# One quarter of two weight units split into 16 partitions and four transfers of eight partitions

## The chip, the core and the metric

The kernel runs on one core of one Trainium2 chip. The metric is device time in microseconds (us) of one execution. The core has TensorE (PE, matmuls), VectorE (DVE), ScalarE (ACT), GpSimd (POOL) and SyncE (SP). Sixteen DMA engines move data between HBM and the on-chip memory SBUF (128 partitions). POOL and SP each issue transfers into a queue of their own, and the same sixteen engines serve all queues.

## The reference

Causal attention with a decaying bias over 8 batches, 8 heads, 576 tokens and head size 64; then a mix of 64 Fourier modes along the tokens, with a complex 512 by 512 weight matrix for each mode; then a residual with one more product.

```python
scores = scale * np.matmul(q, k.transpose(0, 1, 3, 2))
cum = np.cumsum(np.maximum(s, 0.0), axis=-1)
bias = -(cum[:, :, :, None] - cum[:, :, None, :])
scores = np.where(causal, -1000000000.0, scores + np.minimum(bias, 0.0))
attn_out = softmax(scores) @ v
x = attn_out.transpose(0, 2, 1, 3).reshape(8, 576, 512)
X = np.fft.rfft(x, axis=1)
Xr, Xi = (np.real(X[:, :64]), np.imag(X[:, :64]))
Yr = np.einsum('bmd,mde->bme', Xr, w_r) - np.einsum('bmd,mde->bme', Xi, w_i)
Yi = np.einsum('bmd,mde->bme', Xr, w_i) + np.einsum('bmd,mde->bme', Xi, w_r)
y = np.fft.irfft(Y, n=576, axis=1)
u = x + y
out = u + np.maximum(u @ w_ch, 0.0)
```

The weights `w_r` and `w_i` are 64 by 512 by 512 in float32, 67 MB each. They are read once and stored on chip as bfloat16.

## The kernel before, in words

**Steps.** The attention runs in 32 steps n (L725), one for each pair of heads g (four of them) and batch b (eight). A step computes the scores of two heads, their exponentials (ACT, L513), the product with v (L545), and the forward transform of the step before (L567, L586). Products with the mode weights are put between, from step 8 on: `mode_steps` (L320) gives each step its list, and `mode_products` (L709) runs them at L605. Unit 7 is multiplied in step 14 and unit 12 in step 20. After the attention come the products of the last group g (`modes`, L619, matmuls at L628), the inverse transform, the last product and the stores.

**Weights in units.** For the first three groups g, the weights come in 24 units u. A unit holds 16 modes of the real or of the imaginary weights for the 128 rows of g, as a tile of 128 partitions. `unit_loads` (L249) makes the list of its transfers: four quarters h of 32 partitions each, 512 KB in SBUF and 1 MB in HBM. A destination row holds four blocks j of 2048 elements, (q e) with four q and 512 e. The units use five buffers `w_sb` in turn (L118, L234), but for the first two, which use other tiles. The last group comes in 16 smaller pieces (`tile_loads`, L270), each of two transfers of 64 partitions, and the last piece in four.

**Order of the loads.** `loads_w` (L294) hands out the quarters in order, up to a count; `asked[0]` is how many have been handed out. `on_chip[n]` (L337 to L343) is the count for step n: 3n + 2 from step 8 to step 19, and never past a buffer that a product of this or a later step still has to read (`fits`, L326). In each step, `load` (L311) takes the list of q, k and v loads and the list of weight quarters, places the i-th of l entries at (i + 0.5) / l, sorts by that, and issues all of them on POOL (L315). So a POOL instruction that waits (for a buffer, for instance) holds everything behind it. The transfers that POOL issues use eight semaphores in turn, and a transfer waits until the one eight places ahead has landed.

**SP** issues the small row loads of qt (L441, two rows each), the constants Gx and Gt (L773, L777), and after the last load `mark` (L1040), the spreads of y into yv (L662, 16 partitions each) and the stores.

**At the end**, `modes` of the last mode group waits for the last loads of the weights; then come transposes, products and the stores of the results.

Of the kernel before, what the change touches and what calls it, by code (L numbers as in the profile page):

```python
# [19 lines left out]
def kernel(  # L20
# [15 lines left out]
    P = 128  # L36
# [189 lines left out]
    HU = WM * DM  # L226

    def slot(i, x, n=1):

        return w_sb[i][:, x * WM : (x + n) * WM, :].rearrange("p m e -> p (m e)")  # L230
# [8 lines left out]
    def parts_of(u):  # L239

        if u == 0:
            return [(0, xg[:, : 4 * HU])]
        if u == 1:
            return [(0, ya[:, HU:]), (3, xg[:, 4 * HU : 5 * HU])]
        return [(0, slot(UNIT_AT[u], 0, 4))]

    wt = {}

    def unit_loads(u):  # L249

        g, c, ri = u // NCK, u % NCK // 2, u % 2
        src = (moe_w_r, moe_w_i)[ri][:, g * P : (g + 1) * P, :]
        slots, todo = [], []
        for j0, t in parts_of(u):
            slots += [t[:, i : i + HU].rearrange("p (q e) -> p q e", q=QD) for i in range(0, t.shape[1], HU)]
        for h in range(QD):
            todo.append([])
            for j0, t in parts_of(u):
                first = 1 if ri == 1 and c + h + j0 == 0 else 0
                j1 = j0 + t.shape[1] // HU  # L260
                todo[-1].append((
                    t[QP * h : QP * h + QP, first * HU :].rearrange("p (j x) -> p j x", x=HU),
                    src[16 * c + 4 * (j0 + first) + h : 16 * c + 4 * j1 - 3 + h : 4].rearrange(
                        "j (p q) e -> p j (q e)", q=QD
                    ),
                ))
        wt[g, c, ri] = slots
        return todo

    def tile_loads(k):  # L270

        c, ri = divmod(k, 2)
        src = (moe_w_r, moe_w_i)[ri][:, (NG - 1) * P :, :]
        i, x = TILE_AT[k]
        t = slot(i, 2 * x, 2).rearrange("p (m e) -> p m e", e=DM)
        m0 = 2 * MC * (c // 2) + 2 * (c % 2)
        todo = []
        for x0, x1 in [(0, 4)] if k < NT3 - 1 else [(0, 2), (2, 4)]:
            for h in range(2):
                first = 1 if ri == 1 and c == 0 and x0 + h == 0 else 0  # L280
                todo.append((
                    t[HP * h : HP * h + HP, 2 * (x0 + first) : 2 * x1].rearrange("p (m q) e -> p m (q e)", q=2),
                    src[m0 + 4 * (x0 + first) + h : m0 + 4 * x1 - 3 + h : 4].rearrange(
                        "m (p q) e -> p m (q e)", q=2
                    ),
                ))
        wt[NG - 1, c, ri] = [t[:, :WM], t[:, WM:]]
        n = len(todo) // 2
        return [todo[:n], todo[n:]]

    NLW = 4 * NUN + 2 * NT3
    asked, queued = [0], []

    def loads_w(upto):  # L294
        todo = []
        while asked[0] < min(upto, NLW):
            if not queued:
                t = asked[0]
                queued.extend(unit_loads(t // 4) if t < 4 * NUN else tile_loads((t - 4 * NUN) // 2))
            todo += queued.pop(0)  # L300
            asked[0] += 1
        return todo

    def place_of(t):
# [44 lines left out]
    first = loads_qk(0)  # L349
    load(first[:2])  # L350
    load(loads_w(2 * W0), loads_v(0) + loads_tails(0) + first[2:] + loads_v(1))
    nc.sync.dma_start(out=Ff_sb.rearrange("p T c -> p (T c)"), in_=d_Ff)
    nc.sync.dma_start(out=G_sb[:, :S], in_=d_G)
# [11 lines left out]
    with tc.tile_pool(name="cum_psum", bufs=1, space=PSUM) as cpsum:  # L365
# [29 lines left out]
        for x in range(2):  # L395
            rows = slice(NL * x, NL * x + NL)
# [222 lines left out]
    def modes(g, c, meanwhile=None, ris=(0, 1)):  # L619
# [16 lines left out]
        for x in range(2 * ris[0], 2 * ris[-1] + 2):  # L636
# [3 lines left out]
            for z in range(4):  # L640
                if meanwhile:
                    product(ri, z // 2, 2 * y + z % 2)
                else:
                    product(ri, y, z)
        load(loads_w(fits(NLW, 2 * NUN + 2 * c + ris[-1] + 1)))
        if ris[-1] == 0:
            nc.vector.tensor_tensor(out=y_acc[:, c, :], in0=ps, in1=y_acc[:, c, :], op=ALU.add)
# [68 lines left out]
    with tc.tile_pool(name="sc_psum", bufs=2, space=PSUM) as scpool, \  # L716
# [8 lines left out]
        for n in range(N):  # L725
            tails_due = loads_tails(n // B + 1)[n % B - 3 : n % B - 2] if 2 < n % B < 5 else []
            load((loads_qk(n + LA) if n % 2 else []) + (loads_vs(n) if n else loads_v(LA)) + tails_due, loads_w(on_chip[n]))
            if n == N - B:
                nc.gpsimd.dma_start(out=wch_sb, in_=moe_w_ch.rearrange("(dt p) e -> p dt e", p=P))
# [18 lines left out]
            i = first_pairs[n - N + len(first_pairs)] if n >= N - len(first_pairs) else None  # L748
# [350 lines left out]
    for step in (  # L1099
# [8 lines left out]
        i = int(step[1:].rstrip("ab"))  # L1108
# [34 lines left out]
```

## Time and profile before

| | |
|---|---|
| median of 3 runs | 435.75 us (435.31 to 435.78) |
| the profiled execution's own time | 435.96 us |
| its span, first to last instruction | 434.2 us |
| mean granted TensorE clock | 0.972 |
| busy: PE, DVE, ACT, POOL | 88%, 59%, 57%, 31% |
| bytes moved by the DMA engines | 92.87 MB, mean 214 GB/s |
| HBM read | 163.29 MB |
| POOL's transfers | 199 |
| last load lands | 399.17 us |

The engines' busy time is that of instructions on them. A line of a waits view names the engine and line that waited, what ended the wait, the total in us, the number of waits and the longest. A line of a timeline gives start, duration, engine, line, operation and operands, and in square brackets the idle time before it with what ended that. A line of a windows view gives, for a stretch of time, its length, the busy us of PE, PE's weight loads, DVE, ACT and POOL (instructions in brackets), the granted clock, the DMA engines' busy share and the GB/s that they moved. Each DMA engine that takes part in a transfer adds one to the transfer's semaphore when its part is done. The trace has the time of each of these marks but not the engine's number.

### The profile page before, as it was taken

How to read it: one execution, taken by the hardware profiler on the slowest of the kernel's cores; microseconds unless marked ns; L12 is line 12 of the kernel's file. 1: busy time of each engine (PE TensorE's matmuls, PEld its weight loads, DVE VectorE, ACT ScalarE, POOL GpSimd, SP SyncE). 2: the span in 40 equal slices, each digit the busy share in tenths (PEclk: the TensorE clock that was granted, in tenths of full speed). 3: DMA queues.
4: the chain of work that ended last, by engine and by line, in shares of the span. 5: the costliest groups of instructions: out<-in, count | busy, mean ns of one | idle time of the engine just before them, and what ended most of it. 6: DMA issues, size and time to landing. Idle time of an engine off the chain costs nothing. (4 is left out here: it accounts for less than half of the span.)

```text
span 434.2 us, 12629 instructions
## 1 busy us (share of the span) xinstructions
PE 380.6 (88%) x5395; PEld 220.2 (51%) x5395; DVE 256.5 (59%) x574; ACT 249.5 (57%) x556; POOL 136.5 (31%) x218
## 2 busy tenths in 40 slices
PE   1599999999999999999998898979879777877994
PEld 1256666546666655665665455545544334533441
DVE  7555656526775756667665565554636443671795
ACT  1387777717767765666775356545542343451894
POOL 6463333131333223233322222222222222210582
PEclk9999999989999999999999699998989998999998
DMA  8999999999999999999999999999999999995798
GB/s 157 210 207 210 214 207 209 213 214 210 210 211 211 207 212 214 212 211 208 211 212 212 212 212 211 213 212 214 212 210 212 211 211 211 211 211 103 224 365 316
DMA packets 47105, 92.87 MB, mean 214 GB/s; under 512 B 8222, under 2 KB 17946, under 8 KB 47050
## 3 DMA queue, kind: packets, MB, share of 16 engines
q0 software_dynamic: 40400, 81.28, 99.5%
q1 hardware_dynamic: 6650, 10.80, 7.4%
q8 instruction: 42, 0.69, 0.6%
q14 instruction: 13, 0.11, 0.1%
HBM read 163.29 MB, written 9.51 MB: 398 GB/s over the span
## 5 line engine op out<-in xcount | busy, mean ns | idle before, releaser
L513 ACT ACTIVATE p_sb<-sc_ps,cumt_sb 128x320 f16<-128x320 f32 (+1 forms) x384 | 161.1, 519 | 37.6 <-PE sc_ps L504 37.6
L504 PE MATMUL sc_ps<-qt,kt 128*64 128x256 bf16 (+3 forms) x640 | 95.9, 295 | 2.3 <-ACT kt L458 1.7
L504 PEld LDWEIGHTS <-kt 128*128 128x128 bf16 (+1 forms) x640 | 50.5, 126 | 62.7 <-issue 36.0
L315 POOL DMA_DIRECT2D w_sb<-in_moe_w_i_dram x62 | 35.2, 568 | 88.0 <-DMA w_sb<-in_moe_w_r_dram 32.0
L458 DVE COPY qt<-tr_ps 64x576 bf16<-64x576 bf16 x64 | 47.7, 745 | 18.3 <-PE tr_ps L454 18.0
L550 DVE RECIPROCAL rcp<-av_ps 128x5 f32<-128x5 f32 x64 | 12.4, 194 | 77.9 <-PE av_ps L545 77.9
L315 POOL DMA_DIRECT2D w_sb<-in_moe_w_r_dram x60 | 34.0, 567 | 77.5 <-DMA w_sb<-in_moe_w_r_dram 24.3
L493 PE MATMUL sc_ps<-negm,ident 128*128 128x512 bf16 x128 | 51.0, 399 | 0.0
L545 PEld LDWEIGHTS <-p_sb 128*128 128x128 f16 x1088 | 40.7, 98 | 3.6
L454 PE MATMUL tr_ps<-ident,qk 64*64 64x64 bf16 x1152 | 31.6, 198 | 10.7 <-DVE kt L458 5.2
L475 ACT ACTIVATE p<-sc_ps,cumt 128x64 f16<-128x64 f32 x32 | 10.1, 314 | 53.3 <-PE sc_ps L471 53.3
L458 ACT COPY kt<-tr_ps 64x576 bf16<-64x576 bf16 x32 | 22.9, 716 | 23.7 <-DVE qt L458 23.2
L454 PEld LDWEIGHTS <-qk 64*64 64x64 bf16 x1152 | 24.3, 112 | 23.2 <-DVE kt L458 8.3
L496 PE MATMUL sc_ps<-negm,ident 128*128 128x256 bf16 x128 | 35.9, 281 | 0.0
L545 PE MATMUL av_ps<-va,p_sb 128*128 128x65 f16 x768 | 35.0, 194 | 0.0
L605 PE MATMUL yp<-w_sb,xs 64*32 64x512 bf16 (+1 forms) x704 | 30.9, 414 | 4.3 <-DMA w_sb<-in_moe_w_i_dram 2.3
L551 DVE TENSOR_TENSOR x_all<-av_ps,rcp 128x320 f16<-128x320 f32 x64 | 31.5, 492 | 2.2
L617 DVE TENSOR_TENSOR y_acc<-yp,y_acc 128x512 f32<-128x512 f32 x34 | 21.9, 687 | 14.9 <-PE yp L605 14.9
L545 PE MATMUL av_ps<-vb,p_sb 128*128 128x65 f16 x320 | 26.0, 195 | 0.0
L315 POOL DMA_DIRECT2D vr<-in_v_dram x22 | 15.1, 687 | 31.1 <-DMA w_sb<-in_moe_w_r_dram 8.8
L458 DVE COPY kt<-tr_ps 64x576 bf16<-64x576 bf16 x32 | 24.4, 763 | 0.4
L684 ACT COPY w_sb<-z_ps 128x512 f32<-128x512 f32 x20 | 11.7, 587 | 22.5 <-PE z_ps L703 16.1
(127 smaller groups left out, 539.3 us busy)
## 6 DMA issues: line engine op xcount, KB each, us to landing
w_sb<-in_moe_w_r_dram POOLq DMA_DIRECT2D x60, 512.0 KB, 17.5
w_sb<-in_moe_w_i_dram POOLq DMA_DIRECT2D x55, 512.0 KB, 16.9
out_dram<-w_sb SPq DMA_DIRECT2D x16, 512.0 KB
qk<-in_q_dram POOLq DMA_DIRECT2D x15, 288.0 KB, 13.8
qk<-in_k_dram POOLq DMA_DIRECT2D x15, 288.0 KB, 14.7
vr<-in_v_dram POOLq DMA_DIRECT2D x14, 256.0 KB, 15.5
x_all<-in_moe_w_r_dram POOLq DMA_DIRECT2D x4, 512.0 KB, 9.9
y_acc<-in_moe_w_i_dram POOLq DMA_DIRECT2D x3, 384.0 KB, 7.1
```

Of the source, the lines that this page charges most:

```text
L315: nc.gpsimd.dma_start(out=dst, in_=src)
L454: nc.tensor.transpose(ps[rows, r, :], src[rows, r, :], ident16[rows, rows])
L458: copy(out=to[:, :, :, half * RH : half * RH + RH], in_=ps[HP * i : HP * i + HP].rearrange("d r (h p) -> d h p r", h=2),)
L493: nc.tensor.matmul(ps[:, : 2 * W], ident16, both, start=True, stop=False, skip_group_check=True)
L496: nc.tensor.matmul(ps[:, S : S + W], ident16, negm[:, NMB + m0 : NMB + m0 + W], start=True, stop=False, skip_group_check=True,)
L504: nc.tensor.matmul(ps[rows, c0 : c0 + i1 - i0], keys, qh[:, i0:i1], start=False, stop=True, skip_group_check=True,)
L513: nc.scalar.activation(out=pt[:, o : o + n_], in_=ps[:, c0 : c0 + n_], func=ACTF.Exp, bias=cumt_sb[:, x, pidx : pidx + 1], scale=0.125,)
L545: nc.tensor.matmul(ps[:, I, :NCH], lhsT, rhs, start=(i == 0), stop=(i == len(todo) - 1), skip_group_check=True,)
L550: nc.vector.reciprocal(out=rcp, in_=ps[:, :, D])
L551: nc.vector.tensor_tensor(out=x_all[:, g, b, :, D * h : D * h + D], in0=ps[:, :, :D], in1=rcp.unsqueeze(2).to_broadcast([P, NT, D]), op=AL ...
L605: nc.tensor.matmul(ps[hp][32 * j : 32 * j + 32, :], cols[k0:k1, q_, c0 : c0 + 4 * B, 4 * c + j], wt[g, c, ri][j][k0:k1, q_, :], start=(ri ...
L617: nc.vector.tensor_tensor(out=y, in0=ps[hp], in1=y, op=ALU.add)
```

## The change

Units 7 and 12 no longer load their second quarter (partitions 32 to 63 of the tile) in one transfer. The transfer now covers its first 16 partitions. The other 16 go as four pieces of eight partitions: first partitions 48 to 55 whole; then of partitions 56 to 63 blocks j 0 and 1 of the first 128 columns; then all blocks of columns 128 to 2047; then blocks 2 and 3 of the first 128 columns. The pieces wait in a list. `loads_w` adds a piece to the weights when `asked[0]` reaches a given number: for unit 7, 31, 33, 35 and 39, so behind quarters of units 7, 8, 8 and 9; for unit 12, 51, 53, 55 and 57, so behind quarters of units 12, 13, 13 and 14. The same bytes arrive as before, in eight transfers more on POOL in all.

```diff
+    BEHIND = {7: (1, 3, 5, 9), 12: (1, 3, 5, 7)}
+    pieces = []
     wt = {}
 
     def unit_loads(u):
...
         wt[g, c, ri] = slots
+        if u in BEHIND:
+            (dst, src), = todo[1]
+            todo[1] = [(dst[:16], src[:16])]
+            for i, after in enumerate(BEHIND[u]):
+                rows = slice(24, 32) if i else slice(16, 24)
+                x = slice(0, HU) if i == 0 else slice(P, HU) if i == 2 else slice(0, P)
+                j = (slice(0, 4), slice(0, 2), slice(0, 4), slice(2, 4))[i]
+                pieces.append((4 * u + 2 + after, (dst[rows, j, x], src[rows, j, x])))
         return todo
...
             todo += queued.pop(0)
             asked[0] += 1
+            while pieces and pieces[0][0] == asked[0]:
+                todo.append(pieces.pop(0)[1])
         return todo
```

## The prediction

> **What bounds the kernel now.** I read the page's slices and queues first, then the waits of TensorE, then the timeline at the end of the loads.
>
> ```profile
> span 434.2 us, 12629 instructions
> DMA  8999999999999999999999999999999999995798
> q0 software_dynamic: 40400, 81.28, 99.5%
> q8 instruction: 42, 0.69, 0.6%
> ```
>
> The queue that POOL fills (q0) has packets on the engines for 99.5% of the span's engine time, and the DMA row stands at 9 until slice 36, which is about 400 us. So the transfer engines are the limit up to there. The rest, 35 us, is a tail in which no weight arrives.
>
> ```profile
> PE yp L628 <- DMA w_sb<-in_moe_w_i_dram: 6.9, 7, 1.9
> PE yp L628 <- DMA w_sb<-in_moe_w_r_dram: 3.4, 2, 1.9
> ```
>
> These are TensorE's waits from 330 to 400 us: 10.3 us, each for weights. The last one sets the start of the tail:
>
> ```profile
> 396.74 0.65 PE L628 MATMUL yp<-w_sb,xs 128*32 128x512 bf16 x4 [0.79 <-DMA w_sb<-in_moe_w_i_dram]
> 399.21 0.65 PE L628 MATMUL yp<-w_sb,xs 128*32 128x512 bf16 x4 [0.41 <-DMA w_sb<-in_moe_w_i_dram]
> ```
>
> So what counts is when the **slowest** of the sixteen engines has finished its list. A transfer's semaphore gets sixteen marks, one an engine. Sorted, in us, for POOL's transfers counted from 0 (198 is the last load):
>
> ```
>  66  110.22 110.49 111.24 111.25 111.58 111.63 111.76 111.81 | 111.81 111.83 112.04 112.34 112.43 112.82 112.99 113.77
>  97  172.03 172.16 172.86 173.26 173.53 173.74 173.85 174.37 | 174.56 174.67 174.84 174.88 174.98 175.56 176.15 176.51
> 109  195.96 196.23 196.72 197.33 197.47 197.83 198.10 198.62 | 199.38 199.48 199.50 199.71 199.92 199.98 200.00 200.67
> 198  391.80 392.29 392.52 393.16 393.30 394.13 394.95 396.59 | 397.26 397.36 397.71 397.72 397.73 397.89 398.71 399.17
> ```
>
> The engines are not level. Seven lead, the eighth lies by itself at 396.59, eight trail. An engine's marks repeat at 2.458 us a full quarter, so each engine can be followed. From transfer 152 to 198 each of the trailing eight is set back once by 1.06 to 1.19 us, when q8 (instructions, 16 KB packets) has one. None of the leading eight is, so they are two sets of eight engines, of which one also carries instructions. The small loads of qt, two rows each, set back two engines by 0.06 us; they end at 394.13 and 396.59, both in the leading set.
>
> **The change part by part.**
>
> *The rows moved.* A quarter is 32 partitions, two an engine, and takes an engine 2.46 us, so one row is 1.23. In place of it come 16 partitions (one row on all engines), a large transfer of 8 partitions, a tiny one, a large one (1920 of 2048 columns), a tiny one. The trace of before holds no transfer of 8 partitions, so which engines carry it is open. The two-row loads of qt hit two engines, so I take eight rows on eight engines. Taken by turns, the order large, tiny, large, tiny puts both large ones on the same eight. Those get −1.23 + 1.23 + 0.94 × 1.23 = +1.15 us a unit, and four marks more of 0.02 (the 4-byte packets take 22 ns): +1.23. The others get −1.23, two tiny ones of two 256-byte runs (such packets take 31 ns in the loads of Ff_sb, so some 0.05 each), the marks 0.08: −1.05. Over units 7 and 12: **+2.46 and −2.10**.
>
> If the large ones fall on the leading set, the seven end by 394.95 + 2.46 = 397.41, the trailing eight by 399.17 − 2.10 = 397.07, and the eighth at 396.59 + 2.46 = 399.05. The last load lands at 399.05 for 399.17: **−0.12 us**. The levelling works on fifteen engines and is given back by one. If they fall on the trailing set, the end is 399.17 + 2.46 = 401.63: +2.46. These are the two ends of this term. [...]
>
> [...]
>
> *Narrow writes.* Sixteen rows, or eight, take the writes of many engines into few partitions. The nearest row is the spread of yv, 16 partitions each time, beside the steady stretch:
>
> ```profile
> 172.00:192.00 20.00, 19.84 (x360) 12.40 (x359) 14.20 (x33) 13.71 (x32) 5.93 (x10) 1.00 1.12 211
> 402.00:404.40 2.40, 2.25 (x20) 0.99 (x19) 1.40 (x4) 1.28 (x3) 0.00 (x0) 1.00 0.78 98
> ```
>
> The last column is GB/s: 211 in the loads, 98 in the spread. At 98 a 16-partition transfer (256 KB) takes 2.7 us for 1.23, and at half of it a large one (128 KB) on eight engines 2.7 for 1.23: +1.4 each, three a unit, two units, 8.2 us on the engines that carry all of them (2.8 on the others). That is the upper bound and holds if all engines come to the rows together. The lower bound is 0, and a gain is excluded, since nothing in the edit makes a row of weights faster. The engines pass a load within 3.55 us at transfer 66 and 4.48 at 97, a row takes 1.23, so a minority overlap. I take a sixth of the bound, **+1.3 us** on the eighth engine.
>
> [...]
>
> *The late pieces.* The last tiny one of unit 12 is issued behind unit 14's first quarter (transfer 109), unit 12's product needs it, and TensorE works in order:
>
> ```profile
> 193.60 1.11 PE L605 MATMUL yp<-w_sb,xs 64*32 64x512 bf16 x32
> ```
> ```profile
> 182.33 0.59 POOL L315 DMA_DIRECT2D qk<-in_q_dram  x1 [1.04 <-PE ft_ps L586]
> 184.65 0.56 POOL L315 DMA_DIRECT2D w_sb<-in_moe_w_r_dram  x1 [1.72 <-DMA w_sb<-in_moe_w_r_dram]
> ```
>
> Transfer 109 is issued at 184.65 and lands at 200.67. Less 2.10 on the engines relieved by then, plus the tiny piece, that is 198.7: unit 12's product starts 5.1 us late. Unit 7's waits likewise behind transfer 81 (landed 141.20): 140.2 for 139.63, +0.6, which is inside the 5.1. Behind the product stand the transposes of the next step, then scores, av and fft, and the qk slot that they free. What hides it are TensorE's later waits, from 190 to 330 us:
>
> ```profile
> PE tr_ps L454 <- DMA qk<-in_k_dram: 3.4, 2, 2.1
> PE yp L605 <- DMA w_sb<-in_moe_w_i_dram: 2.3, 1, 2.3
> PE yp L605 <- DMA w_sb<-in_moe_w_r_dram: 0.7, 1, 0.7
> ```
>
> 6.4 us, and then the 10.3 us above. This holds if the late TensorE doesn't starve the queue: POOL's qk load at 198.32 waits for tr_ps and would go at some 203.4, while the engines have work until 203.12 to 207.86 (the marks of transfer 114), −2.10 or +2.46. That is just enough. **0**, and 5.1 us if the cover is gone.
>
> *Issues.* Eight more on POOL at 0.56 us: 4.5 us, on an engine busy 31%. POOL issues a transfer only when the eighth before it has landed (its eight semaphores in turn), and the small ones take places: two full ones fewer in flight at the worst, 4.9 us of
>
> ```profile
> DMA to landing us min/median/max: 10.9/17.1/20.1
> ```
>
> At POOL's longest wait for TensorE (7.9 us, to 111.86) the foremost engine had 4.9 us of work left; the set with one row less keeps 3.7. In the step that issues transfer 81 the weights now go ahead of q's load instead of behind it. No cost. SyncE's queue gets nothing new; its mark waits for the last load as before.
>
> *Sum.* −0.12 + 1.3 + 0 + 0 = +1.2 us on the profiled execution's 435.96 (its span 434.2 and 1.8 around it): 437.1. The median of the runs is 435.75, 0.21 below it: **436.9 us**.
>
> **The rivals.**
>
> *No change.* Engines pass the narrow rows one by one, and the sum is −0.12: 435.6. For it: the engines' spread of 3.5 to 4.5 us. Against it: in transfer 66 thirteen of them lie within 2 us.
>
> *Faster.* The eighth engine's place is an accident of few events. It lies 1.64 us behind the seventh, of which 0.45 came at one mark at 336 us beside an instruction packet of q14, and the step from the seventh to the eighth mark was 0.05 us at 66, 0.52 at 97 and 109. If the packets fall elsewhere, the end goes to the others', 397.41: −1.76, so 434.0 us. It decides from an eighth engine under 396.0 before the shift. Against it: it is behind in a row from transfer 150 to 198.
>
> *The other set.* The large pieces load the engines that trail: +2.46 and some narrow cost, 438.2 to 439. For it: nothing in the trace tells where eight rows go. Against it: the two-row loads.
>
> *A starved queue.* If the qk load comes too late, up to 5.1 us follow: 440.9. The margin is worked out above, and I give it no chance of its own beside the slower cases.
>
> **How the numbers follow.** Slower by the eighth engine and narrow rows 0.36 (own range 436.6 to 438.3), the other set 0.14, no change 0.24, faster 0.26. Slower together 0.50. About 0.2%, 0.87 us, is what a measurement of this kernel can tell from no change. The range runs from the faster case, 434.0, to the other set, 438.8; the upper bound of the narrow rows and the starved queue are left outside.
>
> **What would show it.** The sixteen marks of the last load: fifteen within 397.5 and one at 399 or later confirms the levelling and the eighth engine; the trailing eight over 400 means the other set; all by 397.5 the faster case. The narrow rows show as marks of the 16-partition transfer more than 1.23 us behind the load before it. Unit 12's product should start at about 198.7 instead of 193.6, with a wait for a load ahead of it, and TensorE's waits for qk and weights between 230 and 320 should shrink by as much. I am wrong altogether if the end of the loads and the end of the span part by more than 0.5 us.

## The result, and the profile after

The changed kernel takes 443.12 us (median of 6 runs, 440.82 to 443.79) beside 436.01 us of the kernel before (435.31 to 437.76): a ratio of 1.0146, 95% interval 1.0119 to 1.0173. It is slower, by 7 us where 1.2 were forecast, and outside the range. The six runs lie in two groups, 440.82 and 441.09 us, and four from 443.11 to 443.79; the profiled execution (443.12 us) is of the upper group, so what is worked out below holds for that one, and no trace shows the lower. The lines named below are 12 higher than before (L327 for L315, L617 for L605).

The GB/s of the page before, then the page after:

```profile
GB/s 157 210 207 210 214 207 209 213 214 210 210 211 211 207 212 214 212 211 208 211 212 212 212 212 211 213 212 214 212 210 212 211 211 211 211 211 103 224 365 316
```
```profile
span 441.3 us, 12640 instructions
DMA  9999999999999999999899999999999999996598
GB/s 163 208 209 210 210 211 208 213 215 203 206 207 212 211 212 202 202 199 160 159 212 213 215 211 211 210 213 214 214 211 212 211 211 211 211 211 126 198 363 319
q0 software_dynamic: 40784, 81.28, 98.7%
```

A slice after is 11.03 us. The row of GB/s has two things to see. Slices 15 to 17 (165 to 199 us) run at 199 to 202 instead of some 211. Slices 18 and 19 (199 to 221 us) fall to 160 and 159: two slices that lack a quarter of their bytes are some 5 us of a queue with nothing in it. The busy share of a DMA engine hardly shows it (one digit 8 among the nines ahead of the tail), and q0's 98.7% is only 0.8 points under the 99.5% of before.

TensorE's waits from 190 to 330 us after, the stretch whose waits were to hide the late product:

```profile
PE yp L617 <- DMA w_sb<-in_moe_w_r_dram: 6.6, 2, 5.2
...
PE yp L617 <- DMA w_sb<-in_moe_w_i_dram: 2.9, 1, 2.9
...
PE tr_ps L466 <- DMA qk<-in_k_dram: 0.6, 1, 0.6
```

The 6.6 us are new: unit 12's product waits 1.4 us for the second large piece and 5.2 for the last tiny one. The other waits for loads are 3.5 us in place of 6.4, so TensorE did give back some of its lateness as forecast. It didn't help, because the loads themselves stood still. POOL's timeline there, the first line from before:

```profile
198.32 0.60 POOL L315 DMA_DIRECT2D qk<-in_q_dram  x1 [2.98 <-PE tr_ps L454]
```
```profile
200.86 0.69 POOL L327 DMA_DIRECT2D v<-in_v_dram  x1 [1.45 <-DMA w_sb<-in_moe_w_i_dram]
210.46 0.59 POOL L327 DMA_DIRECT2D qk<-in_q_dram  x1 [8.91 <-PE tr_ps L466]
211.04 0.57 POOL L327 DMA_DIRECT2D w_sb<-in_moe_w_r_dram  x1
```

POOL holds one qk load for 8.91 us and everything behind it. Before, it held the same load for 2.98 us. The marks around it (transfer 122 is the v load at 200.86, 123 the qk load; sorted, us):

```
122  204.7 ... 207.4 | 207.6 ... 211.2     mean 207.83
123  213.98 ... 214.15 | 214.19 ... 214.42 mean 214.17
```

In a full queue the marks of a qk load follow those ahead of it by 1.39 us (in the kernel before, 1.15 to 1.42 us over the q and k loads from 44 to 140). Here the mean steps by 6.34: **each engine has stood still 4.95 us on average**. And the sixteen, 6.5 us apart ahead of the gap, all start level behind it.

The way from the late product to that load, in TensorE's timeline after:

```profile
198.62 0.54 PE L617 MATMUL yp<-w_sb,xs 64*32 64x512 bf16 x4 [1.39 <-DMA w_sb<-in_moe_w_r_dram]
204.32 1.93 PE L617 MATMUL yp<-w_sb,xs 64*32 64x512 bf16 x28 [5.16 <-DMA w_sb<-in_moe_w_r_dram]
206.18 0.69 PE L466 MATMUL tr_ps<-ident,qk 64*64 64x64 bf16 x18
...
209.69 0.47 PE L466 MATMUL tr_ps<-ident,qk 64*64 64x64 bf16 x18
```

and the same two groups of transposes before, where the product started at 193.60:

```profile
194.64 0.47 PE L454 MATMUL tr_ps<-ident,qk 64*64 64x64 bf16 x18
...
197.54 0.47 PE L454 MATMUL tr_ps<-ident,qk 64*64 64x64 bf16 x18
```

The qk slot is free after the second group. From the product to the issue it took 198.32 − 193.60 = 4.72 us before and 210.46 − 204.32 = 6.14 after: 28 matmuls take 1.93 us where 32 took 1.11. A view by stretches after (length, busy us of PE, PE's loads, DVE, ACT, POOL, then granted clock, DMA share, GB/s) tells why; its first line is from before:

```profile
206.00:209.00 3.00, 2.92 (x65) 2.01 (x65) 2.73 (x9) 2.48 (x6) 1.41 (x3) 1.00 1.19 210
```
```profile
193.00:198.00 5.00, 4.23 (x73) 2.77 (x70) 2.72 (x7) 4.05 (x10) 1.25 (x2) 1.00 1.16 190
198.00:202.00 4.00, 0.54 (x4) 0.24 (x5) 0.00 (x0) 0.15 (x1) 1.25 (x2) 0.92 1.10 205
202.00:206.00 4.00, 1.68 (x28) 0.69 (x27) 0.00 (x0) 0.00 (x0) 0.00 (x0) 0.50 1.16 195
206.00:209.00 3.00, 3.00 (x34) 1.37 (x30) 2.70 (x5) 0.29 (x2) 0.00 (x0) 0.63 0.63 87
209.00:212.00 3.00, 3.00 (x64) 2.06 (x63) 2.05 (x8) 2.98 (x8) 1.54 (x3) 1.00 0.19 21
```

The granted clock is 0.50 when the product's last piece arrives. The trace has it at 0.50 from 201.4 to 208.2 us and full from there to 324.3; the 0.92 and 0.63 are means over both. DMA moves 87 and then 21 GB/s in the stretches in which POOL waits. The half clock begins 2.2 us into the wait of 5.16 us and ends 3.9 us behind the product's start at 204.32.

The end. The last load lands at 404.96 (399.17 before, +5.8), and the sixteen marks lie within 3.6 us (7.4 before):

```
401.4 401.5 401.7 401.8 401.8 401.9 402.4 402.9 | 403.5 403.5 403.7 403.8 403.8 404.0 404.7 405.0
```

The span grew by 7.1, so 1.3 us more are lost behind the loads. TensorE's last products after:

```profile
403.06 0.67 PE L640 MATMUL yp<-w_sb,xs 128*32 128x512 bf16 x8
404.64 0.65 PE L640 MATMUL yp<-w_sb,xs 128*32 128x512 bf16 x4
406.63 0.65 PE L640 MATMUL yp<-w_sb,xs 128*32 128x512 bf16 x4
```

Before, the last product waited for its load and started 0.04 us behind it. Here it starts 1.67 us behind with no wait ahead of it: TensorE is late by itself. Its longest wait in the last stretch and the clock behind that:

```profile
PE yp L640 <- DMA w_sb<-in_moe_w_i_dram: 5.5, 3, 2.6
```
```profile
384.00:388.00 4.00, 3.08 (x28) 1.56 (x29) 1.89 (x3) 0.00 (x0) 0.77 (x2) 0.71 1.13 212
388.00:392.00 4.00, 3.27 (x33) 1.44 (x35) 0.00 (x0) 1.18 (x3) 1.00 (x2) 0.50 1.12 210
```

Before, the clock was 1.00 in both stretches.

### The profile page after: what moved, and what is told of

Its sections match the earlier page's. It is cut to its first block, busy times and chain, and to the rows that moved or that the text cites. A ratio compares the mean times of both kernels' runs of the same rounds, so it can differ in the third digit from the quotient of the medians.

```text
span 441.3 us, 12640 instructions
## 1 busy us (share of the span) xinstructions
PE 382.7 (87%) x5395; PEld 220.4 (50%) x5395; DVE 256.3 (58%) x574; ACT 248.8 (56%) x556; POOL 140.9 (32%) x226
## 3 DMA queue, kind: packets, MB, share of 16 engines
q0 software_dynamic: 40784, 81.28, 98.7%
## 5 line engine op out<-in xcount | busy, mean ns | idle before, releaser
L516 PE MATMUL sc_ps<-qt,kt 128*64 128x256 bf16 (+3 forms) x640 | 94.9, 293 | 2.4 <-ACT kt L470 1.7
L327 POOL DMA_DIRECT2D w_sb<-in_moe_w_i_dram x66 | 37.6, 570 | 88.9 <-DMA w_sb<-in_moe_w_i_dram 30.3
L327 POOL DMA_DIRECT2D w_sb<-in_moe_w_r_dram x64 | 36.3, 567 | 81.6 <-DMA w_sb<-in_moe_w_r_dram 30.9
L617 PE MATMUL yp<-w_sb,xs 64*32 64x512 bf16 (+1 forms) x704 | 33.0, 434 | 12.9 <-DMA w_sb<-in_moe_w_r_dram 6.6
L617 PEld LDWEIGHTS <-xs 64*32 64x32 bf16 (+1 forms) x768 | 16.4, 141 | 24.9 <-issue 16.8
L327 POOL DMA_DIRECT2D qk<-in_q_dram x17 | 10.5, 616 | 45.6 <-PE tr_ps L466 34.9
```

Of the source, the lines that this page charges most:

```text
L327: nc.gpsimd.dma_start(out=dst, in_=src)
L516: nc.tensor.matmul(ps[rows, c0 : c0 + i1 - i0], keys, qh[:, i0:i1], start=False, stop=True, skip_group_check=True,)
L617: nc.tensor.matmul(ps[hp][32 * j : 32 * j + 32, :], cols[k0:k1, q_, c0 : c0 + 4 * B, 4 * c + j], wt[g, c, ri][j][k0:k1, q_, :], start=(ri ...
```

## The experiments

The theory now: **two causes**. Writes into few consecutive partitions take the engines longer (*narrow*), and the pieces that are asked for late hold unit 12's product, then TensorE, then the qk load, until the queue is dry (*late*). Rivals: the one or the other alone does it. For each run the mean delay of the sixteen marks against the kernel before is taken at the same load, counted as before: 95 (between the units), 112 (ahead of the qk load that waited), 115 (the qk load), 198 (the last). "Slowest" is the last mark of the last load (399.17 before).

```
                        95     112     115     198   slowest  time us   ratio [95%]
the change             0.20    2.04    7.01    7.18   405.0   443.12   1.0146 [1.0119, 1.0173]
e_early                2.00    5.22    5.21    6.12   405.5   441.10   1.0119 [1.0081, 1.0157]
e_only12              -0.23    0.45    5.50    5.69   403.6   441.39   1.0121 [1.0082, 1.0160]
e_late_piece          -0.59   -0.45    2.92    3.08   400.7   438.44   1.0063 [1.0042, 1.0084]
e_early_swap           3.34    5.67    5.56    7.99   410.3   444.62   1.0214 [1.0161, 1.0267]
e_early_stride        -0.32    0.31    0.28    0.80   400.5   437.61   1.0048 [1.0025, 1.0070]
e_only7                0.11    0.34    0.46    0.51   399.4   437.14   1.0032 [1.0016, 1.0049]
e_change_stride       -0.57   -0.20    5.73    6.02   404.1   442.81   1.0136 [1.0103, 1.0169]
e_early_stride_swap    1.17    2.44    2.18    3.56   405.1   441.76   1.0134 [1.0110, 1.0157]
e_early_stride7       -0.32   -0.10   -0.10    0.78   399.7   436.12   1.0005 [0.9980, 1.0030]
e_early_stride7_swap   0.82    0.68    0.59    1.59   402.2   439.28   1.0080 [1.0053, 1.0107]
```

A step between 112 and 115 is the dry queue; what has come up to 112 is what the engines lost to the pieces themselves. Up to load 95 e_only12 and e_late_piece issue what the kernel before issues, and they stand at −0.23 and −0.59 there: each row is one execution, and differences of under some 0.6 us between such means can't be told.

### The pieces asked for early

```diff
-    BEHIND = {7: (1, 3, 5, 9), 12: (1, 3, 5, 7)}
+    BEHIND = {7: (1, 2, 3, 4), 12: (1, 2, 3, 4)}
```

> The change with its pieces issued right behind units 7's and 12's own quarters (asked 31, 32, 33, 34 and 51, 52, 53, 54), so that none comes after the first two quarters of the next unit. Starved queue (the loss is the late landing of unit 12's last pieces, the product that waits for them, the qk load held behind it and the engines that run dry): unit 12's product starts within 1 us of 193.6, POOL's wait for tr_ps near 198 us is under 4 us, the engines never run dry, and the time is 435 to 437. Narrow writes (the loss is engine time in the transfers of 16 and 8 partitions): the rows are the same, so it stays at 440 to 443.

441.1 us. The dry stretch is gone (no step at 115), and the engines still end 6.1 us later. The page:

```profile
GB/s 161 209 209 208 212 209 209 213 213 202 202 194 209 200 213 198 200 179 210 210 204 203 214 211 212 209 212 215 214 210 211 211 211 211 212 211 100 220 377 305
q0 software_dynamic: 40784, 81.28, 100.1%
```

q0 is never empty (100.1%), but moves 194 to 202 GB/s in several slices about unit 7 and 179 about unit 12. So the pieces, with no dry queue, can cost 5.1 us of the change's 7.1. How much of that is the narrow writes, e_early_stride shows below.

### Unit 12 alone

```diff
-    BEHIND = {7: (1, 3, 5, 9), 12: (1, 3, 5, 7)}
+    BEHIND = {12: (1, 3, 5, 7)}
```

> Only unit 12 is split, as in the change. Starved queue: the loss is all in unit 12, so 440 to 443 with a POOL wait for tr_ps of 7 us or more near 200 us. Narrow writes, shared by the two units: half the loss, 438 to 440, and no dry engines.

441.39 us. Five of its 5.7 us come at one step, the qk load:

```profile
208.90 0.59 POOL L327 DMA_DIRECT2D qk<-in_q_dram  x1 [10.68 <-PE tr_ps L466]
```

Unit 12 carries most of the change; what came before it was not needed to run the queue dry.

### Unit 7 alone

```diff
-    BEHIND = {7: (1, 3, 5, 9), 12: (1, 3, 5, 7)}
+    BEHIND = {7: (1, 3, 5, 9)}
```

> Only unit 7 is split, as in the change. Starved queue: unit 7's late piece holds its product by 2.6 us as in the changed kernel, later waits of TensorE hide that, the engines never run dry: 435.3 to 436.8. Narrow writes, shared by the units: 438 to 440.

437.14 us, 0.32% over the kernel before, and in neither range. There is no dry stretch, and the 0.5 us of engine time can't be told from nothing. The slowest mark is only 0.2 us later than before; in the profiled execution the last product starts 1.81 us behind its load, so most of what is lost there lies behind the loads (see "The end" below).

### A late piece without narrow writes

Unit 12's second quarter keeps its 32 partitions; its first 128 columns go as one transfer of 32 partitions, asked for where the change puts its last tiny piece.

```diff
         wt[g, c, ri] = slots
+        if u == 12:
+            (dst, src), = todo[1]
+            todo[1] = [(dst[:, :, P:], src[:, :, P:])]
+            pieces.append((57, (dst[:, :, :P], src[:, :, :P])))
         return todo
...
             asked[0] += 1
+            while pieces and pieces[0][0] == asked[0]:
+                todo.append(pieces.pop(0)[1])
```

> No narrow transfer at all: unit 12's second quarter keeps its 32 partitions, but its first 128 columns go in a transfer of their own where the change's last piece goes (asked 57). Starved queue from lateness alone: unit 12's product starts at about 200.7, when the load before the piece has landed, TensorE is 7 us late, the qk load of 198.3 goes at 205, at which time the foremost engines have run dry (203.1 in the run before) and the last have not (207.9), so 1 to 4 us more: 437 to 440. Narrow writes: no loss, 435.5 to 436.5.

438.44 us. TensorE and POOL:

```profile
200.34 2.06 PE L612 MATMUL yp<-w_sb,xs 64*32 64x512 bf16 x32 [7.53 <-DMA w_sb<-in_moe_w_r_dram]
```
```profile
206.44 0.60 POOL L322 DMA_DIRECT2D qk<-in_q_dram  x1 [9.31 <-PE tr_ps L461]
```

The queue runs dry here too, by 3.3 us an engine (the same sum: the mean step less 1.39). So a late piece does it with no narrow write at all.

### Sixteen partitions, consecutive or every second one

The second quarter of twelve units (3 to 18 without 8, 9, 16 and 17) goes as two transfers of 16 partitions, one behind the other. First consecutive, then strided:

```diff
+            todo[1] = [(dst[:16], src[:16]), (dst[16:], src[16:])]
```
```diff
+            todo[1] = [(dst[::2], src[::2]), (dst[1::2], src[1::2])]
```

> Twelve units have their second quarter in two transfers of 16 consecutive partitions, one right behind the other; nothing is late and no engine gets more than before. Narrow writes: if each such pair costs 1.0 us of engine time (unit 12 lost about 2 us over its narrow transfers), the end of the loads moves by some 12 us: 445 to 449. If a pair costs nothing: 435.5 to 436.8.

446.52 us, ratio 1.0238 [1.0203, 1.0274], in the range for a pair that costs. Over the twelve that is 0.87 us a pair, and the mean of the last marks is 8.4 us later, 0.70 a pair.

> As the kernel with twelve quarters in two transfers of 16 partitions, but each transfer takes every second partition of the 32. If consecutive partitions are what costs: 435.5 to 436.8, whatever the consecutive form took. If the count of partitions costs: as the consecutive form.

436.61 us, ratio 1.0013 [0.9998, 1.0029]; 0.05 us a pair, the mean of the last marks 0.2 us later. The same bytes, the same number of transfers, the same rows: only which partitions lie in one transfer differs, and with them which rows of HBM one transfer reads. These two runs don't part the writing from the reading side, so "narrow writes" stays a name for what such transfers cost, whichever side it is.

### Early and strided

```diff
-            todo[1] = [(dst[:16], src[:16])]
+            todo[1] = [(dst[::2], src[::2])]
-                rows = slice(24, 32) if i else slice(16, 24)
+                rows = slice(3, 32, 4) if i else slice(1, 32, 4)
```

on top of the early places.

> As the early kernel, but the 16 partitions are every second one of the 32 and the eight are every fourth. If narrow writes cost because consecutive partitions share a way into memory, their cost goes: 0.5 to 3 us under the early kernel, and under before if the levelling works (434 to 435.5). If the cost hangs on the number of partitions alone, or there is none, within 0.5 us of the early kernel.

437.61 us against 441.1: 3.5 us less, more than the 0.5 to 3 expected, and still not under the kernel before, so no gain of the levelling shows. Most of what the early pieces cost was which partitions they took. Up to load 112 the engines lose 0.31 us where they lost 5.22.

### The other order of large and tiny

Tiny, large, tiny, large in place of large, tiny, large, tiny; early, with consecutive partitions.

```diff
-                x = slice(0, HU) if i == 0 else slice(P, HU) if i == 2 else slice(0, P)
-                j = (slice(0, 4), slice(0, 2), slice(0, 4), slice(2, 4))[i]
+                x = slice(0, HU) if i == 1 else slice(P, HU) if i == 3 else slice(0, P)
+                j = (slice(0, 2), slice(0, 4), slice(2, 4), slice(0, 4))[i]
```

(and the rows, so that the whole piece keeps its partitions).

> As the early kernel, but the pieces in the order tiny, large, tiny, large. If transfers of eight partitions go by turns to two sets of eight engines, the large ones now load the other set. If the change's order loads the leading engines, this one loads the trailing ones: the last load lands 2 to 4 us later than with the early kernel and the sixteen marks of the last load lie 10 us or more apart. If the change's order already loads the trailing ones, this one levels the engines: the marks within 4 us and the time 1 to 2 us under the early kernel. If eight partitions always go to the same engines, both times agree within 0.5 us.

444.62 us. The last load's marks spread over 10.5 us instead of 6.5, and the slowest is 410.32 instead of 405.51. So the order does decide how late the slowest engine is, and the change's own order is the cheaper one. That the large pieces go to the set that leads in the one order and to the set that trails in the other, eight each, is less sure: in this run and the two with this order below, six marks lie apart at the end and not eight (the gap behind the tenth is 3.7, 4.0 and 2.6 us).

### The change's places, strided

The stride edit on the change itself: the fourth corner of the square.

> The change with its own places for the pieces, but the 16 partitions are every second one and the 8 partitions every fourth one of the quarter (as in e_early_stride, which took 437.61 us with the pieces asked for early). It is the fourth corner of a square: consecutive or strided partitions, pieces early or late. Theory of two causes that add: the engines lose little to narrow writes here, and the late pieces still hold unit 12's product; its last piece lands some 200 us instead of 204.3, and the queue runs dry before the qk load behind it, with some 2 us, as in e_late_piece: 438.5 to 440. Rival, the late pieces cost something only because narrow writes had made all engines late first: no dry stretch, POOL's longest wait for tr_ps under 6 us, and 437.0 to 438.0 as e_early_stride.

442.81 us. Both theories missed: the first gave at most 440, the second 438. Two of the six runs, 439.72 and 439.86 us, do lie in the first one's range; the other four, and the profiled one with them, lie at 442.8 to 443.4. The narrow writes are gone (−0.20 at load 112), and the dry stretch is longer than in the change, 5.90 us an engine. TensorE's and POOL's timelines, and the clock:

```profile
202.02 1.93 PE L617 MATMUL yp<-w_sb,xs 64*32 64x512 bf16 x28 [3.70 <-DMA w_sb<-in_moe_w_r_dram]
```
```profile
198.31 0.69 POOL L327 DMA_DIRECT2D v<-in_v_dram  x1 [1.02 <-DMA w_sb<-in_moe_w_i_dram]
209.28 0.59 POOL L327 DMA_DIRECT2D qk<-in_q_dram  x1 [10.28 <-PE tr_ps L466]
```
```profile
206.00:209.00 3.00, 3.00 (x33) 1.36 (x31) 1.27 (x4) 2.06 (x6) 0.00 (x0) 0.50 0.22 30
```

The last piece lands 2.3 us earlier than in the change, but the clock stays at 0.50 until past 209, and the way from product to qk load takes 7.26 us instead of 4.72. The load goes 1.2 us earlier than in the change, and engines that were not slowed by narrow writes simply wait longer for it. **The two causes don't add**: what narrow writes cost ahead of the gap, the gap takes back.

### Early, strided, the other order; and unit 7 alone in both orders

> e_early_stride with the order tiny, large, tiny, large. The order decides which set of eight engines carries the large pieces (in e_early and e_early_swap it moved the spread of the last load from 6.5 to 10.5 us). Theory: here too, so the trailing set gets 2.46 us more and the leading set 2.1 us less; the last load lands some 2 us after e_early_stride's 400.5, and the time is 439 to 440. Rival: with strided partitions the sets are not what the order says (e_early_stride's own spread of 8.0 us shows no levelling), and the time stays within 0.6 us of 437.6.

441.76 us, and the slowest mark is at 405.14 instead of 400.48: the theory held in kind, but the mark is 4.7 us later and not some 2, and the time went past its 440.

> e_early_stride for unit 7 alone. One row more on the set that leads in the kernel before, one less on the set that trails, hardly any narrow cost, no late piece. Theory: half of e_early_stride's 1.6 us over the kernel before: 436.5 to 437. Rival, the levelling of one row is worth more than the narrow writes cost: the trailing eight end 1.05 us earlier (397.36 to 398.1 instead of 399.17), 434.8 to 435.6.

436.12 us, no difference that can be told (the interval holds 1). It lies under the theory's 436.5, and the rival's gain didn't come.

> e_early_stride_swap for unit 7 alone: the row goes to the other set of eight engines. If the order decides the set, and the sets of the kernel before are what the end of its loads shows, the last load lands some 1.2 us later than in the kernel before: 437 to 437.8. If e_early_stride7 comes out slower than this one, the set that the order large first loads is the trailing one once the partitions are strided.

439.28 us, over the expected 437.8; the slowest mark is 2.42 us behind that of e_early_stride7. So no version beats the kernel before.

## Why the prediction was wrong, step by step

**What bounds the kernel** held: the loads set the end, and every run's time follows the slowest mark and what lies behind it.

**The rows moved** held in kind: the order of large and tiny pieces decides how late the slowest engine is, and the change's order is the cheaper. That the large pieces meet on the same eight engines, and on the leading ones, as the sum's −0.12 takes it, was the author's assumption, and no run shows which engines carry them; what the runs showed in its place is the slowest mark 4.8 us later in the other order for two units (410.32 against 405.51). The sizes didn't hold, though they seem to. The step gave one set +1.23 us a unit and the other −1.05, so the trailing eight should end 2.28 us a unit apart in the two orders. Measured between the slowest marks: 410.32 − 405.51 = 4.8 and 405.14 − 400.48 = 4.7 for two units (4.56 by the step), 402.16 − 399.74 = 2.4 for one (2.28). But at load 130 they are only 1.5, 1.8 and 0.5 apart, and at load 138 3.1, 5.0 and 2.0. In between lies load 136, of `wch_sb`, at which the mean mark steps by 3.53, 3.35 and 3.21 us in the tiny-first order and by 2.58 to 2.76 in the change's (2.64 before). A large part of the agreement is therefore luck; why that load takes longer there is open. The level failed too. By the step the slowest would be at 398.1 in e_early_stride7 and was at 399.74, and in e_early_stride it would be the eighth engine at 399.05 (the trailing eight at 397.1) and was 400.48; the other order lies above its own value by 1.8 and 3.5. No run separates what this is. In the change itself the levelling counts for nothing at the end, since the dry queue sets all engines level at 214 us; what counts is how late the slowest engine is ahead of it, since the late piece waits for that one.

**The narrow writes** were put between 0 and 8.2 us, and "a sixth of the bound", 1.3, was taken, because a minority of engines was to meet in the same rows. The bounds held, the choice failed. Early, they cost 5.22 − 0.31 = 4.9 us of engine time up to load 112, and 3.5 us of the time (441.1 against 437.61). At the change's own places they cost 2.04 + 0.20 = 2.2 us of engine time up to there; this size is loose, since e_only12, with the same pieces of unit 12, stands at 0.45. Why later places cost less is open. The runs show that the cost hangs on which partitions share a transfer, 0.87 us a pair for 16 consecutive ones and 0.05 for every second one; by what mechanism, no run shows. The upper bound that the prediction gave for level engines, 8.2 us, was not reached; that it is because the engines are not level is argued and not shown.

**The late pieces** are the step that failed: put at 0 with "that is just enough", measured as 4.95 us of idle engines (5.90 without the narrow writes, 3.3 for a late piece with none). The change's cost is mostly there: without the narrow writes it is still 7.1 us over its kernel before (442.81 against 435.72). These shares are not what taking one cause away would save, since without the lateness 5.1 us are left as well (e_early). Four things were wrong in the step.

- *Where the piece lands.* It was put at 198.7: 200.67 for transfer 109, less 2.10 us for relieved engines, plus the piece. The same loads stand ahead of the piece as were landed with transfer 109 before; the q load has only changed places with the quarter. But the product waits for the slowest engine (in the change the piece's last mark is at 204.27 and the product starts at 204.32), and that one was not relieved: at load 109 the slowest mark is 1.1 us later than before in e_change_stride and 3.4 in the change with its narrow writes, where 2.1 earlier was forecast. So 201.98 and 204.27 instead of 198.7.
- *The way from there to the qk load* was taken as before, 4.72 us. TensorE's clock fell to 0.50 during the wait, and the way took 6.14 (7.26 in e_change_stride). Landing and clock take the forecast 203.4 to the measured 210.46: 5.6 + 1.4.
- *The margin* set the issue of the load beside the engines' marks. But the load issued at 210.46 had its first packet at 211.75, and with idle engines its first mark came 3.5 us behind the issue (213.98 − 210.46), of which 1.39 is what such a load takes in a full queue. So by the author's estimate 2.1 us belong to the margin, and 203.4 would already have left the foremost engines idle.
- *The cover*, 6.4 us of TensorE's later waits, hides a late TensorE, and not a queue that stood still. It is no cover for what bounds the kernel.

The rival "a starved queue" was therefore the right one, and was given no chance of its own. Its 5.1 us were near the idle time by another sum: the product's delay, which was 10.7 us in the end, less what the engines still had to do.

**Issues**: 0 is in keeping with e_split16_stride, twelve issues more for 0.13% (0.9998 to 1.0029).

**The end.** The prediction called itself wrong altogether if the end of the loads and the end of the span part by more than 0.5 us, and they part by 1.3. Across the fourteen profiles, where the granted clock between 380 and 404 us is 1.00 the last product starts 0.04 to 0.05 us behind the last load. In all six where it is 0.79 to 0.93 it starts 0.5 to 3.2 us behind (the change 1.67, e_only12 3.15, e_change_stride 2.72, e_early_swap 2.04, e_only7 1.81, e_late_piece 0.52). What sets the clock there was not tried by a run of its own.

So of 7.1 us of span, 5.8 are the last load's (a mean of 7.2: 2.0 up to load 112, 4.95 at the dry queue and 0.2 behind it, the levelled spread taking some back at the slowest), and 1.3 a slower TensorE behind it.

## What to carry to other kernels

Where a queue of loads bounds the time, ask of every late-landing piece which issue it holds up, not which product: follow it through the engine that works in order to the load that waits for that engine's slot, and count when the slowest engine will have landed the piece, the clock after the wait (0.50 here) and the time from issue to first mark (3.5 us here). A wait on the compute engine that costs nothing by itself is dear when the issuing engine waits behind it: here one of 5.16 us on TensorE stood ahead of one of 8.91 on POOL, and the engines idled for 4.95 on average. If a transfer of 32 partitions must be split, try every second partition before blocks of consecutive ones (0.05 us a pair here against 0.87).

## What the runs showed that was not expected

- Which partitions share a transfer mattered more than how many transfers there were: 0.87 us a pair for blocks of 16, 0.05 for every second partition.
- The dry queue was a leveller: 6.5 us between the first and last engine ahead of the gap, 0.44 behind it. In e_late_piece the engines lose 3.1 us on average, and the slowest only 1.5.
- With a wait of 3.7 us (e_change_stride) TensorE stood at half its clock for longer than with one of 5.2 us (the change): from 201.0 to 211.3 us in the one, from 201.4 to 208.2 in the other. The earlier landing was partly given back that way, 7.26 us against 6.14 to the qk load. In the traces of the kernel before and of the change every stretch at one clock that ends inside the trace lasts a whole number of steps of 3.41 us (3.41, 6.83, 47.79 and 116.05 among them), and the one of e_change_stride lasts three (10.2). So the length of the wait alone does not set how long the clock stays low. Work behind the wait does not set it alone either: in e_change_stride TensorE was busy for all 5.00 us from 204 to 209 at a clock of 0.50, and the full clock came 9.3 us behind the product's start at 202.02, in the change 3.9 us behind it. What does set it no run here shows.
